# Rewriting a block-causal attention kernel that feeds a hash-routed mixture of experts

## The chip, the cores and the metric

The kernel runs on one core of a Trainium2 chip. The metric is the device time of one launch in microseconds (us). All times of the trace come from one profiled execution; the times of the kernel come from separate runs.

## What is computed

Two stages follow each other. q, k and v have 8 batches, 8 heads, 576 positions and 64 dimensions, in fp32. Attention is causal by blocks of 64 positions: position i sees position j if i // 64 >= j // 64. The result x, 4608 tokens by 512, goes to one of 8 experts per token; the token's id decides which.

```python
scores = scale * np.matmul(q, k.transpose(0, 1, 3, 2))
mask = (pos[:, None] // 64) >= (pos[None, :] // 64)
attn = softmax(np.where(mask, scores, -1e9))
x = np.matmul(attn, v).transpose(0, 2, 1, 3).reshape(4608, 512)
expert_idx = token_ids * np.int64(2654435761) % np.int64(8)
for e in range(8):
    m = expert_idx == e
    out[m] = np.maximum(x[m] @ w1[e], 0.0) @ w2[e]     # 512 -> 1024 -> 512
```

The multiplier is 1 modulo 8, so the expert is the token id modulo 8. In the inputs used here the experts have 565, 591, 525, 624, 619, 579, 546 and 559 tokens.

## The kernel before

The code has three stages, each in its own pools; the order within an engine is that in which a scheduler of the language places what the code lists, and the waits between engines come from the tiles that instructions share.

**Routing (lines 96 to 177).** The token ids are loaded four times 1152, repeated on 8 partitions (L121), one partition per expert. DVE and ACT compute the id modulo 8, a one-hot row and its running sum (L124 to L142); 72 small matmuls turn the slots to token order (L145). 36 indirect DMAs on POOL write token numbers into `perm_dram` (L171); each writes the same tensor, so each waits for the one before it. L177 reads the table back into `perm3`. An expert has 6 x 128 = 768 slots; empty ones hold the number 4608.

**Attention (L200 to L393), per batch.** SP loads q, k and v (L203 to L216); DVE casts them to bf16 (L220 to L226). PE transposes 128-row chunks of q and k by matmuls with an identity (L244, L250) into one PSUM tile, DVE and ACT copy the results out (L266, L270). Scores are computed transposed, keys by queries, per head and 128 keys, only for queries at or after them (L285, L290); ACT takes the exponential into `PT` (L302) and DVE zeroes the quarter that the block mask forbids (L308). Then PV (L351) has `PT` as the stationary side and v with a column of ones as the moving one, so the row sum comes out as column 65; DVE divides (L360 to L373). Heads go in pairs, PV of a pair after the scores of the next. SP writes x in token order to `x_dram` (L386, L391).

**Experts (L403 to L494).** The weights of an expert are loaded and cast to bf16 by POOL's DMAs (L415, L417); the pools of this stage take over the memory of attention's. For each 128 slots an indirect DMA gathers rows of x (L425), PE transposes them (L431) and DVE copies them (L435). Stage a (L446, L452) makes the hidden layer, stage b (L460, L467) the output, which an indirect DMA scatters to the tokens' rows (L468). Each such scatter writes `out`, and waits for the one before it. Experts overlap: stage a of e, then weights and gathers of e + 2, then stage b of e - 1.

Of the kernel before, what the change touches and what calls it, by code (L numbers as in the profile page):

```python
# [9 lines left out]
_PAIRINTER = _os.environ.get("BCA_PAIRINTER", "0") == "1"  # L11
_KCOPY_DVE = _os.environ.get("BCA_KCOPY_DVE", "0") == "1"
_SKIP_MOE = _os.environ.get("BCA_SKIP_MOE", "0") == "1"
_SKIP_ATT = _os.environ.get("BCA_SKIP_ATT", "0") == "1"
_SKIP_S0 = _os.environ.get("BCA_SKIP_S0", "0") == "1"
_SKIP_PV = _os.environ.get("BCA_SKIP_PV", "0") == "1"
_SKIP_TR = _os.environ.get("BCA_SKIP_TR", "0") == "1"
_PVN = int(_os.environ.get("BCA_PVN", "65"))
ALU = mybir.AluOpType
ACT = mybir.ActivationFunctionType  # L20
F32 = mybir.dt.float32
BF16 = mybir.dt.bfloat16
I32 = mybir.dt.int32
I64 = mybir.dt.int64


@with_exitstack
def kernel(
# [13 lines left out]
    B, H, S, D = q.shape  # L42
    N_tok = B * S
    E, Dm, FF = moe_w1.shape
    assert D == 64 and Dm == H * D
    assert S % P == 64 and (2 * S) % P == 0, "kernel assumes S = n*128 + 64 (e.g. 576)"
    BLK = 64
    assert (H * S) % P == 0
    NC = (H * S) // P
    NPAIR = H // 2  # L50
    assert H % 2 == 0
    NQT = (S + P - 1) // P
    NCHUNK = N_tok // P
# [38 lines left out]
    if _SKIP_S0:  # L92
        SEC = 0
# [431 lines left out]
```

## Time and profile before

| what | us |
|---|---|
| median of 3 runs (646.69 to 651.3) | 647.71 |
| profiled execution, first to last instruction | 643.9 |
| difference of the two | 3.8 |
| PE busy | 500.3 |
| ACT busy | 254.1 |
| DVE busy | 244.1 |
| POOL busy | 148.1 |

Busy times of different engines overlap. A matmul's busy time holds its latency, so neighbours overlap too. "Idle before" in a row is time in which that engine had nothing to do, with what ended it.

### The profile page before, as it was taken

Reading aid. Unit: us, or ns where it says so; the run is one execution under the profiler, and the core shown is the slowest. Engines: PE = TensorE matmul, PEld = TensorE weight load, DVE = VectorE, ACT = ScalarE, POOL = GpSimd, SP = SyncE. Lnnn points to the kernel's source line nnn. Section 1 sums busy time; section 2 is a strip of 40 time slices with the busy share of each in tenths; the row PEclk is TensorE's granted clock in tenths of the full one; section 3 lists DMA queues with packets and bytes.
Section 4 is the critical chain, followed back from the end, with each engine's and each line's share of the span. In section 5 each row is a group of like instructions: output and inputs, shape, how many; then the busy total and the mean of one; then the engine's idle time right before and its main releaser. Section 6 shows DMA issues by size and latency. Waiting matters only on the chain. (4 is left out here: it accounts for less than half of the span.)

```text
span 643.9 us, 8321 instructions
## 1 busy us (share of the span) xinstructions
PE 500.3 (78%) x3144; PEld 274.4 (43%) x3144; DVE 244.1 (38%) x823; ACT 254.1 (39%) x589; POOL 148.1 (23%) x160
## 2 busy tenths in 40 slices
PE   0426899999999999999999147879596969699850
PEld 0424454545555454555545024435252525354420
DVE  5575555464645546464444011122212121212210
ACT  3422556556565655656566004314040404043100
POOL 1001431222300000000000344441525262422232
PEclk9999999999999999999999999789898989899996
DMA  7499008356190835610010699655565655251101
GB/s 157 83 215 211 7 2 194 65 121 138 53 208 1 192 68 126 133 45 1 2 38 1 123 199 203 141 130 115 125 127 124 132 124 123 71 112 66 57 37 55
DMA packets 81065, 66.44 MB, mean 103 GB/s; under 512 B 41790, under 2 KB 73055, under 8 KB 80994
## 3 DMA queue, kind: packets, MB, share of 16 engines
q1 hardware_dynamic: 61122, 33.33, 24.9%
q0 software_dynamic: 19904, 32.59, 23.7%
q8 instruction: 24, 0.39, 0.3%
q14 instruction: 15, 0.12, 0.1%
HBM read 68.48 MB, written 17.35 MB: 133 GB/s over the span
## 5 line engine op out<-in xcount | busy, mean ns | idle before, releaser
L302 ACT ACTIVATE PT<-sc_ps 128x576 bf16<-128x576 f32 (+4 forms) x320 | 132.4, 435 | 100.8 <-PE sc_ps L285 70.5
L285 PE MATMUL sc_ps<-qkT 64*128 64x512 bf16 (+4 forms) x320 | 132.0, 438 | 10.4 <-ACT PT L302 8.2
L452 ACT ACTIVATE hT<-hp 128x256 bf16<-128x256 f32 (+1 forms) x128 | 61.9, 490 | 181.2 <-PE hp L446 180.1
L351 PE MATMUL Oall<-vext,PT 128*128 128x65 bf16 (+2 forms) x960 | 106.3, 245 | 2.1
L460 PE MATMUL yp<-w2b,hT 128*128 128x512 bf16 x384 | 96.7, 406 | 9.2 <-DVE ysb L467 9.2
L351 PEld LDWEIGHTS <-PT 128*128 128x128 bf16 (+2 forms) x960 | 67.5, 129 | 74.7 <-DVE PT L308 24.1
L446 PE MATMUL hp<-xT,w1b 128*128 128x256 bf16 (+1 forms) x512 | 95.6, 334 | 1.9 <-ACT hT L452 0.8
L266 DVE CAST qkT<-pt 64x512 bf16<-64x512 f32 (+7 forms) x128 | 58.1, 454 | 48.9 <-PE pt L250 34.1
L468 POOL DMA_INDIRECT out_dram<-ysb,perm x48 | 48.0, 999 | 116.0 <-DMA out_dram<-ysb,perm 68.0
L467 DVE COPY ysb<-yp 128x512 f32<-128x512 f32 x48 | 33.2, 691 | 98.6 <-PE yp L460 45.9
L244 PE MATMUL pt<-identbf,qb 128*64 128x128 bf16 (+1 forms) x320 | 65.0, 302 | 5.5 <-ACT qkT L270 5.2
L171 POOL DMA_INDIRECT perm_dram<-tok,f_i x36 | 37.1, 1031 | 137.2 <-DMA perm_dram<-tok,f_i 81.9
L446 PEld LDWEIGHTS <-w1b 128*128 128x128 bf16 x512 | 50.5, 99 | 42.4 <-issue 11.4
L435 DVE COPY xT<-tp 128x512 bf16<-128x512 bf16 x48 | 19.9, 424 | 125.3 <-PE tp L431 125.0
L431 PE MATMUL tp<-identbf,xg 128*128 128x128 bf16 x192 | 20.6, 246 | 59.1 <-DMA xg<-x_dram,perm 58.9
L250 PE MATMUL pt<-identbf,kb 128*64 128x128 bf16 (+1 forms) x320 | 65.0, 299 | 0.0
L460 PEld LDWEIGHTS <-hT 128*128 128x128 bf16 x384 | 39.4, 104 | 57.1 <-issue 22.1
L270 ACT CAST qkT<-pt 64x512 bf16<-64x512 f32 (+7 forms) x128 | 49.8, 389 | 34.2 <-DVE qkT L266 32.2
L425 POOL DMA_INDIRECT xg<-x_dram,perm x48 | 46.3, 965 | 48.1 <-PE tp L431 26.1
L285 PEld LDWEIGHTS <-qkT 64*128 64x128 bf16 (+1 forms) x320 | 34.9, 113 | 44.5 <-issue 26.6
L415 POOL DMA_DIRECT2D w1b<-in_moe_w_dram x8 | 6.7, 840 | 180.8 <-DMA x_dram<-xs 176.0
L145 PE MATMUL slot_ps<-ones_e,cum 8*128 8x1 f32 x72 | 16.0, 348 | 40.1 <-DVE cum L139 40.1
(55 smaller groups left out, 309.4 us busy)
## 6 DMA issues: line engine op xcount, KB each, us to landing
vf_s<-in_v_dram SPq DMA_DIRECT2D x32, 256.0 KB, 5.1
w1b<-in_moe_w_dram POOLq DMA_DIRECT2D x8, 1024.0 KB
w2b<-in_moe_w_dram POOLq DMA_DIRECT2D x8, 1024.0 KB
x_dram<-xs SPq DMA_DIRECT2D x8, 512.0 KB, 3.1
vf_s<-in_v_dram SPq DMA_DIRECT2D x8, 128.0 KB, 4.0
xg<-x_dram,perm POOLq DMA_INDIRECT x48
out_dram<-ysb,perm POOLq DMA_INDIRECT x48
perm_dram<-tok,f_i POOLq DMA_INDIRECT x36
```

Of the source, the lines that this page charges most:

```text
L244: nc.tensor.matmul(pt[64 * m : 64 * m + 64, 0, ci * P + p : ci * P + pend], lhsT=qb[p:pend, c, :], rhs=identbf[p:pend, p:pend], start=True ...
L250: nc.tensor.matmul(pt[64 * m : 64 * m + 64, 1, ci * P + p : ci * P + pend], lhsT=kb[p:pend, c, :], rhs=identbf[p:pend, p:pend], start=True ...
L266: nc.vector.tensor_copy(qkT[64 * m : 64 * m + 64, pr, 0, sa:sb], pt[64 * m : 64 * m + 64, 0, ua - gi * 4 * P : ub - gi * 4 * P],)
L270: nc.scalar.copy(qkT[64 * m : 64 * m + 64, pr, 1, sa:sb], pt[64 * m : 64 * m + 64, 1, ua - gi * 4 * P : ub - gi * 4 * P],)
L285: nc.tensor.matmul(sc_ps[p0:p1, 0:w1m], lhsT=kTs, rhs=qkT[rows, pr, 0, qs0 : qs0 + w1m], start=True, stop=True,)
L302: nc.scalar.activation(PT[p0:p1, so : so + W_], sc_ps[p0:p1, 0:W_], ACT.Exp, scale=scale,)
L351: nc.tensor.matmul(Oall[0:trows, qt, 0 : D + 1], lhsT=PT[p0:p1, cst : cst + trows], rhs=vext[p0:p1, h, pc["c"], 0 : D + 1], start=(i == 0) ...
L425: nc.gpsimd.indirect_dma_start(out=xg[:], out_offset=None, in_=x_dram[:, :], in_offset=bass.IndirectOffsetOnAxis(ap=perm3[:, gg : gg + 1], ...
L446: nc.tensor.matmul(hp[:, 0:tw], lhsT=w1b[:, db, ft * P : (ft + 1) * P], rhs=xT[:, db, t0 : t0 + tw], start=(db == 0), stop=(db == NKT - 1),)
L452: nc.scalar.activation(hT[:, ft, t0 : t0 + tw], hp[:, 0:tw], ACT.Relu)
L460: nc.tensor.matmul(yp[:, :], lhsT=hT[:, ft, tt * P : (tt + 1) * P], rhs=w2b[:, ft, :], start=(ft == 0), stop=(ft == NFT - 1),)
L468: nc.gpsimd.indirect_dma_start(out=out[:, :], out_offset=bass.IndirectOffsetOnAxis(ap=perm3[:, e * G + tt : e * G + tt + 1], axis=0), in_= ...
```

## The change

Nearly every line is new. Of the old structure the transposed scores, the ones column, the weight loads and the two-stage experts remain. What it does:

- The program's order is the order of every engine's queue (`manual_schedule`), written out by hand.
- Rows of q and k are read so that a partition holds four neighbouring positions (1 KB runs); v is read to match, in 18 DMAs per batch. The cast of v moves from DVE to POOL.
- Two heads share the 128 partitions: one transpose, one PSUM tile, one copy and one exponential serve both; score matmuls of a chunk alternate between the heads' rows. Positions 512 to 575 of all heads are handled once per batch (`T_rest`, `S_rest`).
- The block mask is a multiplication on POOL.
- Routing works on 128 partitions. Its 40 index scatters, the scatters of x and those of the output are declared independent of each other.
- x is written to its slot, expert by expert, by five indirect scatters per batch; the empty rows of each expert are zeroed first. Weights of experts 0, 1 and 2 are loaded during batches 3, 5 and 7.
- An expert has 640 slots. Its x is read with one transposing DMA; no gather, no transposes on PE. Tokens beyond 640 go to a loop at the end, whose count is read at run time.

The diff is cut to its core (added lines; `SYNC` marks a dependence that is waited for):

```diff
+    def load_qk(b):
+        for t, src in ((qf, q), (kf, k)):
+            nc.sync.dma_start(
+                t[:, 0:32, :].rearrange("p (h c) d -> p h (c d)", h=H),
+                src[b, :, 0:512, :].rearrange("h (p c) d -> p h (c d)", c=4))
...
+    def cast_v(b):
+        nc.gpsimd.tensor_copy(
+            vx[:, :, :, 0:D], vf[:, 0:32, :].rearrange("p (h i) d -> p h i d", h=H))
...
+    def T_pair(g):
+        tp = psT.tile([P, 8, P], BF16, name="tp", tag="tp")
+        for w in range(2):
+            src = casted[b][w]
+            for c in range(4):
+                s0 = (pr * 4 + c) * 2
+                nc.tensor.transpose(out=tp[:, 4 * w + c, :],
+                    in_=src[:, s0 : s0 + 2, :].rearrange("p a d -> p (a d)"), identity=identbf[:])
+        nc.vector.tensor_copy(qk[:, pr, :, 0:512]..., tp[:]...)
...
+    def mm_pair(b, pr, ps, o0, i, q0, n):
+        for m in range(2):
+            rows = slice(64 * m, 64 * m + 64)
+            nc.tensor.matmul(ps[:, m, o0 : o0 + n],
+                lhsT=qk[rows, pr, 1, 128 * i : 128 * i + 128],
+                rhs=qk[rows, pr, 0, q0 : q0 + n], start=True, stop=True)
+    def S_chunk(g, ch):
+        ps = psS.tile([P, 2, 512], F32, name="ps", tag="ps")
+        if ch == 0:
+            mm_pair(b, pr, ps, 0, 0, 0, 512)
+        elif ch == 1:
+            mm_pair(b, pr, ps, 0, 1, 128, 448)
+            mm_pair(b, pr, ps, 448, 0, 512, 64)
+        else:
+            mm_pair(b, pr, ps, 0, 2, 256, 320)
+            mm_pair(b, pr, ps, 320, 3, 384, 192)
+        nc.scalar.activation(ptv[:, :, 512 * ch : 512 * ch + 512], ps[:], ACT.Exp, scale=SCALE)
...
+    def mask(g):
+        for i in range(NT):
+            nc.gpsimd.tensor_scalar(reg, reg, halfm[:, 0:1], 1.0, op0=ALU.mult, op1=ALU.mult)
...
+    def PV(g, m):
+        O = psO.tile([P, 5, D + 1], F32, name="O", tag="O")
+        for t in range(5):
+            for i in range(min(t, NT - 1) + 1):
+                nc.tensor.matmul(O[:, t, :], lhsT=pt[:, o0 : o0 + 128], rhs=vx[:, h, i, :],
+                                 start=(i == 0), stop=(i == t))
...
+        nc.vector.reciprocal(rs[:], O[:, :, D : D + 1])
+        nc.vector.tensor_tensor(out=xs[:, :, h * D : (h + 1) * D], in0=O[:, :, 0:D],
+                                in1=rs[:].to_broadcast([P, 5, D]), op=ALU.mult)
+    def scatter_x(b):
+        for i in range(5):
+            ins = nc.gpsimd.indirect_dma_start(out=x_dram[:, :],
+                out_offset=bass.IndirectOffsetOnAxis(ap=slot_i[0:n, i, b : b + 1], axis=0),
+                in_=xs[0:n, i, :], in_offset=None)
+            nc.gpsimd.nop()
+            for w in x_writes:
+                tc.declare_no_dep(ins.ins, w.ins, reason="rows of different tokens")
+            x_writes.append(ins)
+    def route():
+        nc.sync.dma_start(tid[:], moe_token_ids.rearrange("(b s) -> b s", b=B))
...
+        for i in range(5):
+            for b in range(B):
+                ins = nc.gpsimd.indirect_dma_start(out=perm_dram[:, :], ...)
+                nc.gpsimd.nop()
+                for w in writes:
+                    tc.declare_no_dep(ins.ins, w.ins, reason="rows of different tokens")
...
+        rd = nc.gpsimd.dma_start(perm3[:], perm_dram[:]...)
+        for w in writes:
+            tc.add_manual_dep(rd.ins, w.ins.name, SYNC, reason="all tokens placed")
+    load_qk(0)
+    load_v(0)
+    load_qk(1)
+    for e in range(E):
+        z = nc.sync.dma_start(x_dram[e * CAP + 512 : (e + 1) * CAP, :], zx[:])
+    cast_qk(0, 0)
+    cast_qk(0, 1)
+    T_rest(0)
+    T_pair(0)
+    cast_v(0)
+    route()
+    load_v(1)
+    for g in range(NPAIRS + 2):
+        b, pr = divmod(g, NP)
+        if g < NPAIRS:
+            S_chunk(g, 0)
+            S_chunk(g, 1)
+        if g >= 2:
+            PV(g - 2, 0)
+        if g + 1 < NPAIRS:
+            if pr == NP - 1:
+                T_rest(b + 1)
+            T_pair(g + 1)
+        if g < NPAIRS:
+            S_chunk(g, 2)
+            if pr == 0:
+                S_rest(b)
+            mask(g)
+        if g >= 2:
+            PV(g - 2, 1)
...
+        if pr == 1 and b >= 1:
+            scatter_x(b - 1)
+            if b == 3:
+                load_weights(0)
...
+    def load_x(e):
+        r = nc.sync.dma_start_transpose(out=xT[:], in_=x_dram[e * CAP : (e + 1) * CAP, :])
+        for w in x_writes:
+            tc.add_manual_dep(r.ins, w.ins.name, SYNC, reason="all tokens placed")
+    def stage_a(e):
+        for ft in range(NFT):
+            for db in range(NKT):
+                for t in range(2):
+                    nc.tensor.matmul(hp[:, t, 0:HC], lhsT=w1b[:, db, ft * P : (ft + 1) * P],
+                        rhs=xT[:, db, t * HC : (t + 1) * HC], start=(db == 0), stop=(db == NKT - 1))
+            nc.scalar.activation(hT[:, ft, :]..., hp[:, :, 0:HC], ACT.Relu)
...
+    n_ov = nc.values_load(ov_i[0:1, 0:1], min_val=0, max_val=OVT)
+    with tc.For_i(0, n_ov, 1) as j:
...
```

The pools: `ps` has three buffers of two PSUM banks, `tp` and `O` one of one bank each; in the expert stage `hp` has two of two banks and `yp` four of one. `pt` has three buffers, q, k and v two each, the weights and `xT` three. In the loop cast_qk(b + 1), load_qk(b + 2), cast_v(b + 1) and load_v(b + 2) are issued at pairs 1, 2 and 3 of batch b. In the expert stage load_x runs two experts ahead, stage b of e - 1 follows stage a of e, and then come the weights of e + 2.

## Rows read from the trace of the kernel before

**Rows 1.** Stretches: length, busy us (instructions) of PE, PEld, DVE, ACT, POOL; clock, DMA.

```profile
0.00:56.40 56.40, 15.99 (x73) 15.65 (x73) 33.74 (x43) 16.32 (x13) 1.80 (x11) 1.00 0.85 161
56.40:357.20 300.80, 281.89 (x1984) 156.38 (x1984) 157.49 (x685) 175.88 (x448) 37.70 (x37) 1.00 0.38 80
357.20:382.10 24.90, 2.63 (x20) 2.08 (x21) 1.67 (x5) 0.00 (x0) 9.55 (x11) 1.00 0.91 182
382.10:628.60 246.50, 199.75 (x1068) 100.30 (x1067) 49.83 (x90) 61.93 (x128) 95.07 (x98) 0.94 0.52 114
```

**Rows 2.** Groups of instructions by shape: busy us, mean ns of one | idle before.

```profile
L285 PE MATMUL sc_ps<-qkT 64*128 64x512 bf16 x64 | 38.3, 599 | 4.7 <-ACT PT L302 3.0 <-DVE PT L308 1.2
L446 PE MATMUL hp<-xT,w1b 128*128 128x512 bf16 x256 | 62.2, 396 | 0.1
L351 PE MATMUL Oall<-vext,PT 128*128 128x65 bf16 (+2 forms) x960 | 106.3, 245 | 2.1
L302 ACT ACTIVATE PT<-sc_ps 128x576 bf16<-128x576 f32 x64 | 41.7, 651 | 25.4 <-PE sc_ps L290 23.6
L302 ACT ACTIVATE PT<-sc_ps 128x192 bf16<-128x192 f32 x64 | 21.1, 330 | 40.2 <-PE sc_ps L285 39.5
L435 DVE COPY xT<-tp 128x512 bf16<-128x512 bf16 x48 | 19.9, 424 | 125.3 <-PE tp L431 125.0
L360 DVE RECIPROCAL rs<-Oall 128x4 f32<-128x4 f32 x64 | 11.7, 183 | 48.6 <-PE Oall L351 47.9
L362 DVE TENSOR_TENSOR xs<-Oall,rs 128x256 bf16<-128x256 f32 x64 | 26.6, 416 | 0.6
L224 DVE CAST vext<-vf_s 128x2048 bf16<-128x2048 f32 x8 | 9.8, 1224 | 0.4
```

**Rows 3.** PE in order of time (start, us, what), and one stretch as in rows 1.

```profile
404.00:410.00 6.00, 5.22 (x22) 2.74 (x23) 1.27 (x3) 1.19 (x2) 2.87 (x3) 0.50 0.98 206
...
404.78 0.61 PE L431 MATMUL tp<-identbf,xg 128*128 128x128 bf16 x4 [3.39 <-DMA xg<-x_dram,perm]
405.18 0.63 PE L446 MATMUL hp<-xT,w1b 128*128 128x512 bf16 x1
...
336.77 0.27 PE L244 MATMUL pt<-identbf,qb 64*64 64x64 bf16 x2
...
219.34 1.17 PE L351 MATMUL Oall<-vext,PT 128*128 128x65 bf16 x13
...
597.77 10.31 PE L460 MATMUL yp<-w2b,hT 128*128 128x512 bf16 x47
```

**Rows 4.** Two of the longest waits (total, times, longest), and the chain's share by line.

```profile
POOL w1b L415 <- DMA x_dram<-xs: 176.0, 1, 176.0
...
POOL perm_dram L171 <- DMA perm_dram<-tok,f_i: 81.9, 35, 7.5
...
DMA out_dram<-ysb,perm 5%; POOLq L520 0%; POOLq L468 0%
```

**Rows 5.** POOL in order of time, with the idle time before each in brackets.

```profile
1.08 0.28 POOL masks.py:199 TENSOR_SCALAR_AFFINE_SELECT identbf<-identbf 128x128 bf16<-128x128 bf16 x1
...
67.02 0.96 POOL L171 DMA_INDIRECT perm_dram<-tok,f_i  x1 [1.43 <-DMA perm_dram<-tok,f_i]
...
364.20 0.98 POOL L425 DMA_INDIRECT xg<-x_dram,perm  x1 [0.31 <-issue]
...
633.59 0.98 POOL L468 DMA_INDIRECT out_dram<-ysb,perm  x1 [2.53 <-DMA out_dram<-ysb,perm]
```

**Rows 6.** DMA at 106 to 116, 366 to 374, 357 to 360.9 and 72 to 96 us.

```profile
DMA packets 4359, 2.14 MB, mean 214 GB/s; under 512 B 2990, under 2 KB 4358, under 8 KB 4358
...
DMA packets 1296, 1.59 MB, mean 199 GB/s; under 512 B 34, under 2 KB 1053, under 8 KB 1296
...
GB/s 0 0 0 0 0 0 74 305 368 347 347 336 357 368 347 326 347 336 347 378 315 273 242 284 242 95 21 0 0 0 0 0 0 0 0 0 0 0 0 0
...
q0 software_dynamic: 288, 0.01, 0.9%
```

More of the change, by code (lines that the diff above doesn't have):

```diff
@@ L24 @@
 I64 = mybir.dt.int64
+ET = mybir.EngineType
+B, H, S, D = 8, 8, 576, 64
+E, DM, FF = 8, 512, 1024
+N = B * S
+NT = 4
+NP = H // 2
+CAP = 640
+G = CAP // 128
+OVT = 32
+NG = E * G + OVT
+SLOTS = NG * 128
+SCALE = 1.0 / float(D) ** 0.5
 @with_exitstack
@@ new lines, with cast_qk @@
+    for z in range(2):
+        pt4 = fix.tile([P, NP * 64 + 64], BF16, name=f"pt4{z}")
+        nc.gpsimd.memset(pt4[:, NP * 64 :], 0.0)
+        pt4s.append(pt4)
+    def cast_qk(b, which):
+        src = loaded[b][which]
+        dst = att.tile([P, 36, D], BF16, name="qb" if which == 0 else "kb",
+                       tag="qb" if which == 0 else "kb")
+        nc.vector.tensor_copy(
+            dst[:, 0:32, :].rearrange("p (r c m) d -> p r m c d", r=NP, c=4, m=2),
+            src[:, 0:32, :].rearrange("p (r m c) d -> p r m c d", r=NP, c=4, m=2),
+        )
+        nc.vector.tensor_copy(dst[:, 32:36, :], src[:, 32:36, :])
+        casted.setdefault(b, {})[which] = dst
@@ new lines, in S_rest @@
+    def S_rest(b):
+        qk = qkTs[b]
+        ps = psS.tile([P, 2, 512], F32, name="ps", tag="ps")
+        for pr in range(NP):
+            for m in range(2):
+                rows = slice(64 * m, 64 * m + 64)
+                nc.tensor.matmul(
+                    ps[rows, m, 64 * pr : 64 * pr + 64],
+                    lhsT=qk[rows, pr, 1, 512:576], rhs=qk[rows, pr, 0, 512:576],
+                    start=True, stop=True,
+                )
+        for m in range(2):
+            rows = slice(64 * m, 64 * m + 64)
+            nc.scalar.activation(pt4s[b % 2][rows, 0 : NP * 64], ps[rows, m, 0 : NP * 64],
+                                 ACT.Exp, scale=SCALE)
@@ new lines, with stage_b @@
+    out_writes = []
+    def stage_b(e, hT):
+        _, w2b = wtiles[e]
+        for tt in range(G):
+            yp = psY.tile([P, DM], F32, name="yp", tag="yp")
+            for ft in range(NFT):
+                nc.tensor.matmul(
+                    yp[:], lhsT=hT[:, ft, tt * P : (tt + 1) * P], rhs=w2b[:, ft, :],
+                    start=(ft == 0), stop=(ft == NFT - 1),
+                )
+            ysb = mo.tile([P, DM], F32, name="ysb", tag="ysb")
+            nc.vector.tensor_copy(ysb[:], yp[:])
+            gg = e * G + tt
+            ins = nc.gpsimd.indirect_dma_start(
+                out=out[:, :],
+                out_offset=bass.IndirectOffsetOnAxis(ap=perm3[:, gg : gg + 1], axis=0),
+                in_=ysb[:], in_offset=None, bounds_check=N - 1, oob_is_err=False,
+            )
+            nc.gpsimd.nop()
+            for w in out_writes:
+                tc.declare_no_dep(ins.ins, w.ins, reason="rows of different tokens")
+            out_writes.append(ins)
```

783 lines of the change are left out of this document (359 added, 424 removed).

## The prediction

> **What bounds the kernel now.** I read the busy time by stage first. It cuts the 643.9 us span into five stretches [rows 1]: 56.4 us in which the tokens are routed and almost nothing else runs, 300.8 us of attention, 24.9 us between the last attention matmul and the first expert matmul, 246.5 us of experts, and a 15.3 us tail. Each has its own limit.
>
> Attention: 94% of the stretch is busy PE, but busy includes the pipeline's latency. The groups by shape tell more [rows 2]: a 512-column score matmul takes 599 ns, a 512-column expert matmul 396 ns. Where the granted clock reads 0.50 (404 to 410 us), the expert matmul takes 0.63 us [rows 3]. So I read attention as running at the 1.2 GHz level, although the stage view prints 1.00 there. PE has about 7 us of streaming in the 9.4 us (300.8 / 32) of each pair of heads; the rest are short waits on DVE and ACT. ACT is the next engine with 5.5 us per pair (175.9 / 32).
>
> Gap and experts: the list of waits shows the serial gears [rows 4]. The weight load waits 176.0 us for the last write of x, because its buffers are those of attention; index scatters wait 81.9 us for one another. The chain that ended last is the output scatters [rows 4], each waiting for the one before it, one every 3.5 us (0.98 and 2.53 [rows 5]). The gathers, with no such wait, go out every 1.3 us (0.98 and 0.31 before it [rows 5]). At the 2.4 GHz level an output matmul of 512 columns comes every (10.31 - 0.40) / 46 = 0.2154 us [rows 3], so PE's own work per expert is 32 x 0.215 + 32 x 0.108 + 48 x 0.215 and 24 transposes, about 22 us: 8 experts need 176 us and take 246.5.
>
> **The change, stretch by stretch.** The sum is made against the profiled 643.9 us; the median of the runs shown is 647.71, so 3.8 us lie around the span and are added at the end. A run differs from a repetition by up to 0.7%, so 1% is about what can be told from no change.
>
> *A. Start to first PV matmul: 56.4 -> 99 us (a loss).* SP issues, in order, q/k of batch 0 (2.36 MB), v of batch 0 (1.18), q/k of batch 1 (2.36) and 1.05 MB of zeros before the token ids. Batch loads run at 214 GB/s, writes of x at up to 340 to 378 GB/s [rows 6]: 5.9 / 0.214 + 1.05 / 0.34 = 31 us, so the ids land near 33 us. DVE then runs the routing chain: some 27 small operations at about 0.2 us and 9 over 320 elements at about 0.45 us (183 ns for 4 elements, 416 for 256 [rows 2]), 9.5 us: 43 us. POOL then issues 40 index scatters. Freed of the wait for each other they should go at the gathers' 1.3 us [rows 5], 52 us: 95 us. The read-back that follows waits for the last landing (2.4 us from issue, [rows 5]), and only behind it in POOL's queue stand the masks of the first pair (1.4 us). PV of pair 0 needs them, and PE's queue is in order, so after the scores of pairs 0 to 2 PE, ACT and DVE stand still: 99 us. Ends: q/k in 1 KB runs at 340 GB/s and scatters at 0.96 us give 77; scatters that still wait for each other (2.4 us each) give 143.
>
> *B. 32 pairs, 300.8 -> 150 us.* Per pair, engine by engine. PE at the 1.2 GHz level: scores 1536 columns per head, the two heads in different rows of the array. Two 64-row matmuls of before do run side by side: x2 in 0.27 us [rows 3], where one of 65 columns takes 0.245 [rows 2]; so 1536 x 0.43 / 512 = 1.3 us, 0.43 being twice 0.2154 (2.6 if they do not overlap). Eight transposes at 0.10 us ([rows 3]: four, then the next instruction after 0.40): 0.8. Thirty PV matmuls at (1.17 - 0.245) / 12 = 0.077 us, 13 of them in 1.17 [rows 3]: 2.3. With the 64-row remainder 0.1: 4.5 us. The same at 2.4 GHz: 2.3. ACT: 0.84 ns per column from the 651 and 330 ns exps [rows 2], so 1.03 us for 1024 columns, three per pair, and 0.2 of remainder: 3.3. DVE: one copy of 1024 columns at twice 424 ns, two reciprocals of 183 ns, two multiplies of about 0.5, a quarter of 2.8 us of q/k casts (two of 2304 elements, at the v cast's 1224 ns for 2048) and 0.15: 3.1 [rows 2]. POOL: four masks of 128 elements; the nearest row is a 128x128 select in place, 0.28 us [rows 5], 1.4 with gaps; the v cast lies between DVE's 1224 ns [rows 2] and 16 selects, 4.5 us, and I take 4.0 plus the remainder, 1.2 per pair; five scatters of x at 1.3 us per batch, 1.6: 4.2. The DMA queues: 3.54 MB per batch at 214 GB/s is 16.5 us, 4.1 per pair, and 2.5 us of x scatters, 0.6: 4.7 without weights. But three batches are loaded during A; what is left is 5 x 16.5 + 8 x 2.5 + 3 x 10.5 (2.1 MB of weights at 199 GB/s [rows 6]) = 134 us. PE and DMA thus come out level. I take 4.7 us per pair, PE's 4.5 and 0.2 for handovers: 150 us. The memsets, the copies on ACT and the second PSUM copies go; they lay beside PE. The scatter burst on POOL (6.5 us per batch) stands ahead of the next pair's mask, which PV needs two pairs later, and the pair time of 4.7 us covers it; at 3.5 us it would show. Ends: ACT's 3.3 plus handover, 3.6 (115 us); score heads one after the other and POOL's casts at their upper end, 6.2 (198 us).
>
> *C. Gap, 24.9 -> 16 us.* The weights are there early. On the path remain the last normalisation 0.8, five scatters 6.5, their landing 2.5, and the transposing load of 0.66 MB. No such DMA is in the trace; at the 340 GB/s of x's writes it is 2 us, at the rate of the weights 3.3, and a landing adds 2 to 3: I take 5. The Trainium skill (Advanced Engine Details and Errata, X-Bar Transpose (TRN2)) states that transposing DMAs are as fast as regular ones at 350 to 400 GB/s; an estimate by that figure is 1.7 us of data, which would take a microsecond or so off the sum; no run here shows it.
>
> *D. Experts, 246.5 -> 141 us.* Capacity 640 instead of 768, no PE transposes: per expert 64 matmuls of 320 columns at 0.135 us and 40 of 512 at 0.2154: 8.6 + 8.6 = 17.3 us, times 8 is 138, and about 3 for the 1.2 GHz level after C's idle time (6 us at 0.50 in [rows 3]). The output scatters no longer wait for each other: POOL needs 1.3 us per tile, PE 1.7. Copies of the output on DVE and Relus of 640 columns (0.7 us) hide. DMA per expert is 10.5 weights + 3 to 5 transposed x + 6 of output, about 20 us for five experts and 9 for the others, 127 of 141: hidden, with little to spare.
>
> *E. Tail, 15.3 -> 8 us.* Copy 0.7, scatter 1.3, landing 2.5 [rows 5], and about 3 for the test of the overflow loop on all engines (no row for it; 0 to 6). No expert of this draw has more than 624 tokens, so the loop's body does not run.
>
> Sum: 99 + 150 + 16 + 141 + 8 = 414, and 3.8 around it: 418 us.
>
> **Rivals.**
> 1. The independence does not reach the queue: scatters still wait for one another. For it: 35 such waits of 2.3 us each [rows 4]. Against: the waits are on named writes, which the change excludes. A becomes 143; the outputs at 3.5 us are 17.5 us per expert, level with PE, and trail by 9: about 470 us.
> 2. The attention pair is slower, 6 us: heads not side by side, or POOL's casts dear and late masks. For it: POOL's elementwise prices are poorly known. 418 + 42 = 460 us.
> 3. PE goes to 2.4 GHz in attention, because the new order leaves fewer pauses, and ACT sets the pair at 3.6 us. Against: DMA has 134 us to do. 418 - 35 = 383 us.
> 4. The transposing load is slow because it moves in small pieces. The small packets of the index scatters cost 288 packets for 0.9% of 16 engines over 24 us [rows 6], 12 ns each; 0.66 MB in 32-byte pieces is 20,480 of them, 15.4 us on 16 engines. With weights and output that is 31 us of DMA per expert, 216 in D instead of 141, and 10 more in C: about 503 us. The Trainium skill (VectorE: DVE Perf Modes, The three transpose paths) lists 1309 ns for one 128x128 block by DMA; taken 20 times, as an estimate, it also is above PE's time per expert; no run here shows it.
> 5. Slower than before: the load goes element by element. Ten scatters of 128 elements lie in those 24 us, 2.7 ns of an engine per element; 327,680 elements are 55 us per expert, 442 in D: about 719 us. It decides from 46 us per load on ((141 + 230) / 8). Against: the call is a transposing DMA of its own, not a copy with a stride. The same section of the Trainium skill names a strided copy as 19 times slower than the crossbar's transpose, and this call as the latter; no run here shows either.
>
> **How the numbers follow.** Forecast 49% (385 to 450 us by the ends of A and B that do not coincide), rival 1 13%, 2 10%, 3 12%, 4 12%, 5 4%. The predicted time is the forecast's 418. Low 355: A at its lower end and rival 3 together, 361, less a little. High 505 takes in rivals 1, 2 and 4. Faster by over 1% holds in all but rival 5: 0.96; of rival 5's 0.04, 0.03 are slower and 0.01, loads of about 46 us, within 1%.
>
> **What would show it.** First PV matmul near 99 us, with POOL's 40 index scatters 1.3 us apart ahead of it and PE idle; if they are 2.4 us apart rival 1 holds. 512-column score matmuls still near 600 ns, starting in twos; near 390 ns is rival 3. Pairs every 4.7 us. A transposing load that lands within 5 us of issue; 15 or more is rival 4. Expert matmuls without pauses, 17.3 us per expert. The forecast is wrong if attention takes under 125 or over 180 us, or if PE waits for x or weights in the experts.

## The result, and the profile after

The changed kernel takes 410.3 us (median of 4 runs, 409.2 to 413.0); the kernel before took 647.2 beside it. The ratio is 0.634 (95% interval 0.631 to 0.637); the prediction was 418 us, range 355 to 505. The profiled execution spans 409.4 us and was timed at 411.0.

The view of stretches, cut at the prediction's own steps A to E (length, busy us and instructions of PE, PEld, DVE, ACT, POOL; clock, DMA share, GB/s), answers to [rows 1]:

```profile
0.00:96.87 96.87, 8.85 (x70) 4.41 (x70) 19.93 (x66) 9.89 (x11) 46.00 (x66) 1.00 0.51 134
96.87:242.09 145.22, 100.98 (x1570) 68.54 (x1570) 82.18 (x195) 89.66 (x102) 112.92 (x189) 0.84 0.76 184
242.09:257.41 15.32, 0.01 (x1) 0.03 (x1) 0.69 (x2) 0.00 (x0) 4.92 (x5) 0.50 0.66 130
257.41:399.40 141.99, 140.15 (x824) 81.59 (x832) 26.98 (x40) 45.06 (x64) 47.59 (x49) 0.99 0.84 169
399.40:409.40 10.00, 0.00 (x0) 0.00 (x0) 0.69 (x1) 0.00 (x0) 1.21 (x2) 0.71 0.10 38
```

| step | before | predicted | after |
|---|---|---|---|
| A start to first PV matmul | 56.4 | 99 | 96.9 |
| B 32 pairs | 300.8 | 150 | 145.2 |
| C gap | 24.9 | 16 | 15.3 |
| D experts | 246.5 | 141 | 142.0 |
| E tail | 15.3 | 8 | 10.0 |

Every length came within 5 us. That does not make every reason right: in the second row PE is busy in only 101 of 145 us at a mean granted clock of 0.84, where the prediction had it busy throughout at the 1.2 GHz level. Which parts of the rewrite brought attention from 300.8 to 145.2 us no run separates. The groups by shape (busy us, mean ns of one | idle before) answer to [rows 2]:

```profile
L230 ACT ACTIVATE pt<-ps 128x1024 bf16<-128x1024 f32 x96 | 93.1, 1028 | 133.5 <-PE ps L210 119.9 <-POOL pt L254 6.3 <-issue 2.2
L254 POOL TENSOR_SCALAR pt<-pt,halfm 128x128 bf16<-128x128 bf16 x128 | 51.6, 420 | 16.5 <-ACT pt L230 15.5
L161 POOL CAST vx<-vf 128x2048 bf16<-128x2048 f32 x8 | 15.1, 1889 | 16.4 <-DMA vf<-in_v_dram 16.4
L210 PE MATMUL ps<-qkT 64*128 64x512 bf16 x64 | 14.6, 455 | 6.6 <-DVE qkT L201 6.3 <-ACT pt L230 0.2
L201 DVE COPY qkT<-tp 128x1024 bf16<-128x1024 bf16 x32 | 21.9, 685 | 10.4 <-PE tp L196 9.2 <-issue 0.7
```

ACT's exponential is priced well (1.03 us). POOL's prices are not: a mask takes 420 ns on average instead of 0.35, and the v cast 1.9 us instead of 4.0. The 512-column score matmul takes 455 ns, a mean of two levels. In order of time, attention shows what happens (start, us, what, idle before in brackets):

```profile
98.24 0.62 PE L196 MATMUL tp<-identbf,qb 128*128 128x128 bf16 x4
...
104.07 0.40 PE L196 MATMUL tp<-identbf,qb 128*128 128x128 bf16 x4 [0.63 <-DVE qkT L183]
...
105.52 0.61 PE L210 MATMUL ps<-qkT 64*128 64x512 bf16 x6
...
114.49 1.05 POOL L302 DMA_INDIRECT x_dram<-xs,slot_i  x1 [0.16 <-DVE xs L290]
114.51 0.62 PE L279 MATMUL O<-vx,pt 128*128 128x65 bf16 x14 [0.47 <-DVE xs L290]
...
120.24 0.90 POOL L302 DMA_INDIRECT x_dram<-xs,slot_i  x1 [0.30 <-issue]
120.54 0.20 DVE L289 RECIPROCAL rs<-O 128x5 f32<-128x5 f32 x1 [2.51 <-remote]
...
121.18 2.12 POOL L254 TENSOR_SCALAR pt<-pt,halfm 128x128 bf16<-128x128 bf16 x6
...
122.55 0.61 PE L196 MATMUL tp<-identbf,qb 128*128 128x128 bf16 x4 [4.17 <-DVE qkT L183]
...
124.06 0.95 PE L279 MATMUL O<-vx,pt 128*128 128x65 bf16 x14
```

Four transposes take 0.62 us at 98.24, as in [rows 3] where the granted clock reads 0.50, and 0.40 at 104.07: in the second pair PE goes over to the 2.4 GHz level. Two heads' score matmuls do run side by side: six of them, 2048 columns, take 0.61 us, and one after the other at 0.2154 us per 512 they would need 0.86.

The five scatters of x hold POOL from 114.49 to 121.14, and the masks come after them. Beside the scatters the reciprocal of a PV that ended at 117.3 starts only at 120.54, after 2.51 us in which DVE did nothing, released by something that the profile does not name ("remote"); PE waits for the copy behind it on DVE and pauses 4.17 us. This is no single case: 13 of the 64 normalisations start over 0.4 us after their matmuls have ended and DVE is free, all of them beside scatters, 19.8 us in all. Before the pause 14 PV matmuls take 0.62 us, after it 0.95. The stretches around it (columns as above) show the granted clock with it:

```profile
104.00:113.00 9.00, 7.99 (x149) 5.52 (x150) 5.85 (x15) 7.80 (x10) 5.77 (x12) 1.00 0.52 156
...
122.00:131.00 9.00, 8.27 (x116) 5.59 (x116) 4.50 (x13) 5.89 (x8) 6.17 (x14) 0.71 0.89 271
```

From one pair's last normalisation to the next the time is, from the second pair on and batch by batch, 4.8, 3.1, 3.0 | 4.0, 9.3, 3.7, 3.0 | 4.1, 8.4, 4.2, 3.0 us, and so on. A pair that nothing disturbs takes 3.0 to 3.1, three exponentials of ACT; the second pair of a batch, behind the burst of scatters, takes 6.5 to 9.3 in six batches and 5.5 in the seventh.

### The profile page after: what moved, and what is told of

The parts are those of the page before. It is cut to its first block, busy times and chain, and to the rows that moved or that the text cites. A ratio compares the mean times of both kernels' runs of the same rounds, so it can differ in the third digit from the quotient of the medians.

```text
span 409.4 us, 6483 instructions
## 1 busy us (share of the span) xinstructions
PE 250.0 (61%) x2463; PEld 154.6 (38%) x2471; DVE 130.5 (32%) x303; ACT 144.6 (35%) x177; POOL 212.6 (52%) x309
## 5 line engine op out<-in xcount | busy, mean ns | idle before, releaser
L230 ACT ACTIVATE pt<-ps 128x1024 bf16<-128x1024 f32 x96 | 93.1, 1028 | 133.5 <-PE ps L210 119.9
L279 PE MATMUL O<-vx,pt 128*128 128x65 bf16 x896 | 46.2, 208 | 71.8 <-POOL pt L254 48.2
L529 PE MATMUL hp<-xT,w1b 128*128 128x320 bf16 x512 | 72.1, 303 | 16.7 <-issue 15.3
L534 ACT ACTIVATE hT<-hp 128x640 bf16<-128x640 f32 x64 | 45.1, 704 | 103.7 <-PE hp L529 103.4
L279 PEld LDWEIGHTS <-pt 128*128 128x128 bf16 x896 | 37.7, 107 | 89.0 <-POOL pt L254 60.3
L529 PEld LDWEIGHTS <-w1b 128*128 128x128 bf16 x512 | 50.3, 99 | 38.7 <-issue 15.4
L254 POOL TENSOR_SCALAR pt<-pt,halfm 128x128 bf16<-128x128 bf16 x128 | 51.6, 420 | 16.5 <-ACT pt L230 15.5
L422 POOL DMA_INDIRECT perm_dram<-tok,prow x40 | 38.6, 966 | 31.8 <-DVE tok L400 19.9
L302 POOL DMA_INDIRECT x_dram<-xs,slot_i x40 | 43.3, 1081 | 17.8 <-issue 9.6
L210 PE MATMUL ps<-qkT 64*128 64x512 bf16 (+4 forms) x320 | 39.1, 341 | 6.8 <-DVE qkT L201 6.3
L290 DVE TENSOR_TENSOR xs<-O,rs 128x320 bf16<-128x320 f32 x64 | 31.5, 492 | 2.2
L201 DVE COPY qkT<-tp 128x1024 bf16<-128x1024 bf16 x32 | 21.9, 685 | 10.4 <-PE tp L196 9.2
L196 PE MATMUL tp<-identbf,qb 128*128 128x128 bf16 x128 | 15.3, 255 | 16.3 <-DVE qkT L183 9.6
L161 POOL CAST vx<-vf 128x2048 bf16<-128x2048 f32 x8 | 15.1, 1889 | 16.4 <-DMA vf<-in_v_dram 16.4
```

The source lines that it names most:

```text
L196: nc.tensor.transpose(out=tp[:, 4 * w + c, :], in_=src[:, s0 : s0 + 2, :].rearrange("p a d -> p (a d)"), identity=identbf[:],)
L210: nc.tensor.matmul(ps[:, m, o0 : o0 + n], lhsT=qk[rows, pr, 1, 128 * i : 128 * i + 128], rhs=qk[rows, pr, 0, q0 : q0 + n], start=True, sto ...
L230: nc.scalar.activation(ptv[:, :, 512 * ch : 512 * ch + 512], ps[:], ACT.Exp, scale=SCALE)
L254: nc.gpsimd.tensor_scalar(reg, reg, halfm[:, 0:1], 1.0, op0=ALU.mult, op1=ALU.mult)
L279: nc.tensor.matmul(O[:, t, :], lhsT=pt[:, o0 : o0 + 128], rhs=vx[:, h, i, :], start=(i == 0), stop=(i == t),)
L290: nc.vector.tensor_tensor(out=xs[:, :, h * D : (h + 1) * D], in0=O[:, :, 0:D], in1=rs[:].to_broadcast([P, 5, D]), op=ALU.mult,)
```

## The experiments

All stages, cut as above, each from one profiled execution. The last column is the median of four runs for the changed kernel and the two combinations, and a single run for the others:

| kernel | set | A | B | C | D | E | time of its runs |
|---|---|---|---|---|---|---|---|
| changed kernel | - | 96.9 | 145.2 | 15.3 | 142.0 | 10.0 | 410.3 |
| masks on DVE | a | 50.3 | 174.8 | 17.2 | 141.3 | 10.0 | 395.2 |
| index scatters late | a | 49.3 | 144.7 | 15.6 | 162.4 | 10.0 | 383.7 |
| q, k of 2 batches only | a | 96.2 | 135.3 | 14.8 | 141.8 | 10.0 | 399.8 |
| two masks | a | 96.7 | 142.4 | 14.8 | 141.2 | 10.0 | 406.7 |
| two masks, q, k of 2 batches | b | 97.8 | 141.9 | 14.7 | 141.4 | 10.0 | 407.5 |
| ids first | b | 84.0 | 145.0 | 14.3 | 142.2 | 10.1 | 397.2 |
| index scatters wait | b | 147.7 | 143.4 | 14.8 | 140.5 | 10.0 | 457.9 |
| plain load, no loop | b | 96.7 | 143.8 | 13.2 | 142.9 | 7.1 | 405.4 |
| two masks, spread | c | 97.0 | 147.7 | 14.9 | 141.4 | 10.0 | 412.6 |
| the same, q, k of 2 batches | c | 96.3 | 142.6 | 14.8 | 141.8 | 10.0 | 407.3 |
| first combination | c | 36.2 | 169.2 | 25.0 | 152.3 | 10.4 | 398.6 |
| second combination | a | 37.8 | 136.0 | 32.1 | 142.5 | 10.0 | 360.5 |

Kernels of one set ran on the same chip (the second combination later, on that of set a). Where the code of attention was not touched B lies between 143.4 and 145.2, so about 2 us is no difference there. But the sets differ in one thing: the late normalisations beside scatters sum to 15 to 20 us in each kernel of set b, as in the changed kernel, to 5 to 9 in set c, and to nothing in set a. B is therefore compared within a set. Set a also says that they are not simply a part of the 145 us: without any of them index scatters late needs 144.7 us and two masks 142.4, but over those runs DVE's casts wait 12.9 and 14.5 us for q and k, against 6.7 in the changed kernel, so one delay may hide behind the other.

**Start: index scatters that wait.**

```diff
-                for w in writes:
-                    tc.declare_no_dep(ins.ins, w.ins, reason="rows of different tokens")
```

> Edit: the 40 index scatters are no longer declared independent of each other, nothing else. Theory (a scatter that must see the one before it landed takes about 2.4 us instead of 1.26): the first PV matmul comes near 143 us instead of 96.9, the rest as it was, the whole about 456. Rival (the declaration does nothing, the spacing of 1.26 us is POOL's own): 409 to 413.

Measured: first PV at 147.7, whole 457.9. POOL's index scatters in this run, in order of time:

```profile
63.36 0.95 POOL L422 DMA_INDIRECT perm_dram<-tok,prow  x1 [1.70 <-DMA perm_dram<-tok,prow]
65.76 0.95 POOL L422 DMA_INDIRECT perm_dram<-tok,prow  x1 [1.45 <-DMA perm_dram<-tok,prow]
```

And in the changed kernel:

```profile
62.26 0.96 POOL L422 DMA_INDIRECT perm_dram<-tok,prow  x1 [0.30 <-issue]
63.52 0.96 POOL L422 DMA_INDIRECT perm_dram<-tok,prow  x1 [0.31 <-issue]
```

This answers to [rows 5]: the wait for a landing goes, 0.30 us of issue stays, and neither wait of [rows 4] is left: 40 scatters are spaced 1.26 us instead of about 2.5. Waiting costs 50.8 us in A; the prediction's rival 1 had 44 there.

**Start: scatters moved, ids first.** In the first kernel the block of fill, 40 scatters and read-back is called behind the last scatter of x; in the second only the load of the ids moves.

```diff
-    route()
+    prow, tok = route()
...
+    place(prow, tok)
     att_ctx.close()
```

> Edit: only the place of the 40 index scatters, their fill and their read-back on POOL is moved, from ahead of the first mask to behind the last scatter of x. Theory: the first PV matmul comes near 48 us instead of 96.9, because nothing else held the masks; the pairs keep POOL's pace, so attention takes about 145 us and ends near 193; the index scatters then run beside the gap and the first experts (50 us), hold the first output scatters and the weights of expert 3 behind them and cost about 14 us there: 410 - 49 + 14 = 375 us. Rival (the start is set by routing on DVE or by loads, not by the scatters on POOL): the first PV matmul stays past 80 us and the whole does not fall below 400.

```diff
+    nc.sync.dma_start(tid[:], moe_token_ids.rearrange("(b s) -> b s", b=B))
     load_qk(0)
     load_v(0)
```

> Edit: only the place of the load of the token ids in SP's queue, from behind the loads of q, k, v and the zeros to ahead of them. Theory (SP's order sets when routing starts): the ids are there when DVE has copied the first transposes at 16.3 us; routing starts at 16.5 instead of 32.0, waits about a microsecond for POOL's iota behind the v cast, and the first PV matmul comes near 83 us instead of 96.9; the whole 396. Rival (what the start gives is taken back by the loads in attention): first PV near 83, the whole 403 to 408. Rival (routing needs something else that comes at 30 us): first PV stays near 97.

Measured: first PV at 49.3 and at 84.0, wholes 383.7 and 397.2. Both steps of A hold: SP's order sets when routing starts, and the masks stand behind the scatters. The first PV matmul, in the changed kernel's order of time:

```profile
95.77 0.58 POOL L433 DMA_DIRECT2D perm<-perm_dram  x1 [1.41 <-DMA perm_dram<-tok,prow]
96.44 1.08 POOL L254 TENSOR_SCALAR pt<-pt,halfm 128x128 bf16<-128x128 bf16 x3
...
96.87 0.70 PE L279 MATMUL O<-vx,pt 128*128 128x65 bf16 x5 [47.29 <-POOL pt L254]
```

Of the 48 us that moving the scatters saves in A, 20 come back in D (14 expected). In order of time, behind the moved scatters and their read-back:

```profile
258.17 1.01 POOL L556 DMA_INDIRECT out_dram<-ysb,perm  x1 [2.29 <-DMA perm<-perm_dram]
...
261.78 5.18 PE L549 MATMUL yp<-w2b,hT 128*128 128x512 bf16 x16 [10.05 <-DVE ysb L554]
272.80 2.58 PE L534 MATMUL hp<-xT,w1b 128*128 128x320 bf16 x9 [5.83 <-DMA w1b<-in_moe_w_dram]
```

The first output scatter goes out only at 258.17, so the output copies and PE stop for 10.05 us, and then 5.83 us for weights that stood behind them on POOL.

**Attention: whose pace?** Masks to DVE; then loads left out; then POOL's instructions merged; then both.

```diff
-            nc.gpsimd.tensor_scalar(reg, reg, halfm[:, 0:1], ...)
+            nc.vector.tensor_scalar(reg, reg, halfm[:, 0:1], ...)
```

> Edit: the four mask multiplications of a pair go from POOL to DVE and stand behind the second head's normalisation; the same values are computed. Theory (POOL sets the pace of attention, by its masks and by the 40 index scatters that stand ahead of them): the first PV matmul comes near 48 us instead of 96.9, but the PV of pair 4 needs the v cast of batch 1, which still stands behind the index scatters, so PE stops again until about 99; from there 28 pairs at DVE's 3.7 us (3.1 and four masks at 0.15) are 104 us, attention ends near 203 and the whole takes about 371 us. Rival (loads by the DMA engines set the pace): attention ends at 215 to 235, the whole takes 385 to 400. Rival (PE's own work sets the pace, 4.5 us per pair): 99 + 28 x 4.5 = 225, the whole 393.

```diff
-                    load_qk(b + 2)
+                    loaded[b + 2] = [loaded[b][0], loaded[b][1], None]
```

> Edit: q and k of batches 2 to 7 are not read; the tiles of batches 0 and 1 are used again, so the scores of the later batches are those of the first two. 14.2 of 66.1 MB of DMA go. Theory (POOL sets the pace of attention): attention keeps 140 to 147 us, the whole 405 to 411. Rival (loads set the pace, 4.1 us per pair of the measured 4.54): attention falls to what POOL, ACT or DVE allow, 105 to 130 us, the whole to 370 to 395.

```diff
-        for i in range(NT):
+        for i in (0, 3):
+            if i == 0:
+                reg = ptv.rearrange("p m (i x j) -> p m i x j", i=3, x=32)[:, :, :, 0:8:2, :]
```

> Edit: the four mask multiplications of a pair on POOL become two, one of 384 elements per partition and one of 128; the same values are computed. Theory (POOL sets the pace, and an instruction has a fixed part: 128 elements take 420 ns, a cast of 2048 takes 1889): 384 elements take about 0.65 us, a pair is 0.6 us shorter on POOL, attention 126 us instead of 145 and the whole 391. If POOL's price is by the element, 384 take 1.26 us and nothing changes. Rival (loads or PE set the pace): POOL's rows get shorter, attention keeps 142 to 146 us.

> Edit: both at once, two mask multiplications instead of four on POOL, and q and k of batches 2 to 7 not read (the tiles of batches 0 and 1 are used again). Alone the first took attention from 145 us to about 140, the second to 135. Theory (POOL and the loads are two limits that lie nearly level, so that removing one only uncovers the other): together they give far more than the sum of 15, attention 112 to 122 us (POOL is left with 15 us per batch, ACT with 13.2), the whole 375 to 387. Rival (each is a small share of one sum): attention 130 us, the whole 394. Rival (PE's 4.5 us per pair are the floor): no less than 140.

Measured: with the masks on DVE the first PV comes at 50.3, and PV then waits 36.1 us for a v cast, as expected; but from 100 us attention needs 125 us, not 104: the theory missed, and the end at 225 us fits both rivals' numbers. The time does not come from a steady pace: batches 3 to 6 take 15.5 to 16.5 us, where index scatters late, of the same set, needs 15.7 to 21.8, and the longest stop, 11.67 us in batch 7, is for a load. In order of time, with the masks on DVE:

```profile
192.08 1.23 DVE L151 CAST qb<-qf 128x2048 bf16<-128x2048 f32 x1 [7.59 <-DMA qf<-in_q_dram]
...
196.08 0.29 DVE L155 CAST qb<-qf 128x256 bf16<-128x256 f32 x1 [2.77 <-DMA qf<-in_q_dram]
...
197.06 0.95 PE L279 MATMUL O<-vx,pt 128*128 128x65 bf16 x14 [11.67 <-DVE xs L290]
```

Against the kernel of the same set whose attention is unchanged (index scatters late, 144.7, though its loads have less of a start) the missing loads of q and k give 9.4 us, to 135.3, between the two theories (140 to 147, or 105 to 130). Two masks instead of four give 2.3, within the rival's 142 to 146 and far from the theory's 126, though 384 elements take 0.74 us on average instead of three times 0.42: POOL is freed and waits longer for ACT (26.9 us instead of 15.5), since the merged mask needs the last exponential. Both together, in set b, give 141.9 against 143.4 to 145.0 there, where 112 to 122 was expected: the theory of two level limits missed, but 15.4 us of late normalisations lie in that run, so it was not decided by it. What these runs have in common is the place of the stops. With q and k of 2 batches only (set a, four masks), in order of time:

```profile
135.79 0.90 POOL L302 DMA_INDIRECT x_dram<-xs,slot_i  x1 [0.30 <-DMA vf<-in_v_dram]
136.74 2.79 POOL L254 TENSOR_SCALAR pt<-pt,halfm 128x128 bf16<-128x128 bf16 x8
137.16 0.11 PEld L279 LDWEIGHTS <-pt 128*128 128x128 bf16 x2 [2.00 <-POOL pt L254]
137.17 1.39 PE L279 MATMUL O<-vx,pt 128*128 128x65 bf16 x14 [1.72 <-POOL pt L254]
```

Here no normalisation is late, and PE stops for the masks behind the last scatter. Over attention PE's loads of stationary data for PV wait 21.7 us for masks in this run, 12.1 in the changed kernel.

**Attention: is it the burst?** This suggests, and does not yet show, that not POOL's sum but its order counts. The scatters are spread, on the last two kernels:

```diff
-        if pr == 1 and b >= 1:
-            scatter_x(b - 1)
+        if b == B and pr == 1:
+            scatter_x(b - 1, range(5))
+        elif b >= 1 and pr in (1, 2):
+            scatter_x(b - 1, range(2 * pr - 2, 2 * pr))
+        elif b >= 2 and pr == 0:
+            scatter_x(b - 2, [4])
```

> Edit: on the kernel with two mask multiplications (attention 143 us from the first PV matmul to the last normalisation, the whole 406.7); the five scatters of x per batch are no longer in one place on POOL but two behind the second pair, two behind the third and one behind the first pair of the next batch (the last batch's stay together). Theory (it is the burst that costs: 6.5 us of scatters, with weights 8.8, hold the masks longer than the two pairs of lead cover at 3.1 us each, and after each pause PE runs the next pairs at the lower clock): attention 124 to 134 us, the whole 388 to 398. Rival (the loads' 134 us set the pace): attention 134 to 140. Rival (POOL's sum or something else sets the pace, the place does not matter): attention 141 to 145, the whole 405 to 409.

> Edit: the same spreading of the scatters, on the kernel with two mask multiplications and without the reading of q and k of batches 2 to 7 (left out; attention 143 us, the whole 407.5, which refuted that POOL's sum and the loads were the two limits). Theory (the burst): with the loads light and the burst gone POOL has 15 us per batch and ACT 13.2, attention 112 to 124 us, the whole 376 to 389. Rival (the burst is not the cause): attention stays at 136 to 145. Against the run with full loads: if the loads bind once the burst is gone, this one is 8 us or more shorter in attention; if not, within 4.

Measured: 147.7 and 142.6, no gain, and 5.1 between the two, which falls between the bounds named for the loads. By attention and by the whole the theory missed both times, and without the loads the rival's 136 to 145 holds. By batches (time from one batch's last normalisation to the next, weights of an expert issued in the fourth, sixth and eighth) it is half right:

| kernel, q and k of 2 batches | the 8 batches, us |
|---|---|
| four masks, scatters together (set a) | 15.6, 15.7, 17.6, 19.2, 15.7, 19.1, 15.7, 17.4 |
| two masks, scatters together (set b) | 14.9, 17.6, 18.9, 19.0, 16.9, 19.3, 17.9, 18.1 |
| two masks, scatters spread (set c) | 14.9, 16.8, 17.2, 15.6, 25.6, 15.6, 23.3, 14.4 |

With the scatters spread six of the eight lie between 14.4 and 17.2, but two rise above 23. Part of that gain over set b is that fewer normalisations are late: in set a, where none is, the scatters stay together and the five batches without weights take 15.6 to 17.6, the three with weights 17.4 to 19.2. In order of time, with the scatters spread:

```profile
150.75 0.83 POOL L444 DMA_DIRECT2D w1b<-in_moe_w_dram  x1
151.55 0.96 POOL L446 DMA_DIRECT2D w2b<-in_moe_w_dram  x1
...
153.66 1.08 POOL L304 DMA_INDIRECT x_dram<-xs,slot_i  x1 [0.18 <-issue]
155.05 1.00 POOL L304 DMA_INDIRECT x_dram<-xs,slot_i  x1 [0.30 <-issue]
...
167.00 0.41 POOL L164 CAST v<-vf 64x256 bf16<-64x256 f32 x1 [7.80 <-DMA x_dram<-xs,slot_i]
167.50 0.93 POOL L256 TENSOR_SCALAR pt<-pt,halfm 128x384 bf16<-128x384 bf16 x2
168.14 0.95 PE L281 MATMUL O<-vx,pt 128*128 128x65 bf16 x14 [7.49 <-POOL pt L256]
```

The cast of v's remainder waits until the scatters of x have landed; in the changed kernel it starts without delay (0.06 us of idle at most). Spreading put two scatters behind 4 MB of weights (fp32 in HBM) in POOL's own DMA queue; the cast went on 12 us after the second of them was issued, the masks stood behind it, and PE paused 7.49 us. With the full loads the same cast goes on 13.5 us after that scatter (155.59 to 169.05). One wait was traded for another, so these two runs do not decide what a spread burst alone would give.

**Gap, experts and tail: transposing load, loop.** Both edits in one kernel:

```diff
-        r = nc.sync.dma_start_transpose(out=xT[:], in_=x_dram[e * CAP : (e + 1) * CAP, :])
+        r = nc.sync.dma_start(xT[:].rearrange("p k c -> p (k c)"),
+            x_dram[e * CAP : (e + 1) * CAP, :].rearrange("(p g) d -> p (g d)", g=G))
...
-    n_ov = nc.values_load(ov_i[0:1, 0:1], min_val=0, max_val=OVT)
-    with tc.For_i(0, n_ov, 1) as j:
```

> Edit: two, in stages that can be read apart. The transposing load of an expert's x becomes a plain load of the same 0.66 MB (left out: the transposition), and the overflow loop behind the experts is left out, with the reading of its count. Theory: the plain load lands 1 to 2 us sooner, so the gap falls from 15.3 to about 14; PE's pauses in the experts (2.7 us) go, 142 to about 139; the tail falls from 10.0 to about 6.5, as the test of the loop costs some 3 us on engines that are done; the whole 401 to 404. Rival (the transposing load is no dearer than a plain one): gap and experts keep 15 and 142. Rival (the tail is the landing of the last scatter and the end of the program): the tail keeps 9 to 10.

Measured: gap 13.2, experts 142.9, tail 7.1, whole 405.4. In the changed kernel, from the issue of the load to the first expert matmul:

```profile
251.24 9.41 SPq L516 DMA_TRANSPOSE xT<-x_dram  x3
257.41 4.83 PE L529 MATMUL hp<-xT,w1b 128*128 128x320 bf16 x24 [15.32 <-issue]
```

With the plain load:

```profile
249.63 1.31 SPq L516 DMA_DIRECT2D xT<-x_dram  x3
253.69 8.48 PE L531 MATMUL hp<-xT,w1b 128*128 128x320 bf16 x41 [13.20 <-issue]
```

6.2 against 4.1 us: transposing costs 2.1 us once, in the gap, and nothing that shows in the experts, whose 142 us did not fall to the 139 expected. The loop's test costs 2.9 us.

**Putting it together.** The first combination has ids first, two masks, spread scatters, 17 index scatters singly between the pairs and 23 behind x.

> Edit: what helped, in one kernel that computes all: token ids loaded first; the 40 index scatters taken from the start, 17 of them singly between the pairs, 23 behind the last scatter of x, beside the gap and the first experts; two mask multiplications; scatters of x spread over the pairs; weights of expert 2 loaded behind the last scatter of x instead of in batch 7. Theory: first PV matmul near 29 us; attention is then bound by the loads (35 MB at 235 GB/s behind the start, 151 us), with POOL at 145 us, and ends near 180; gap 15, experts 142, tail 10: the whole 347 us. Rival (POOL's single index scatters bring the pauses back): attention ends near 195, the whole 362. Rival (23 index scatters behind x hold the first output scatters and the weights of expert 3): experts 150 to 160, the whole 355 to 365.

Measured: 398.6 us, ratio 0.617 (0.612 to 0.622) to the kernel before: a miss by 52. The wait of the v cast came back (up to 11.4 us for scatters of x, up to 12.5 for v itself), the first transposing load took 16.4 us beside the weights of expert 2, and the experts lost 10, in part in two stops of PE (3.7 and 4.1 us) while the last of the 23 index scatters ran and landed. The second takes the masks off POOL and the weights out of the loads' way:

```diff
+        if pr == 3 and b == 6:
+            load_weights(0)
+            load_weights(1)
+        if b == 0:
+            place(1 if pr == 3 else 3)
+        elif b < 7 and pr in (0, 2):
+            place(2 if b < 5 or pr == 0 else 1)
```

> Edit: one kernel that computes all, with POOL taken off the path from exponential to PV: token ids loaded first; masks on DVE (two multiplications, behind the second head's normalisation); the 40 index scatters spread, 10 in batch 0, 4 or 3 in batches 1 to 6, 8 behind the last scatter of x; weights of experts 0 and 1 behind the last v cast, when all loads of q, k and v are under way, those of expert 2 behind the last scatter of x; the five scatters of x of a batch together again. Theory (what set the pace of attention is POOL's queue, in which scatters and a v cast that waits for their landing stand ahead of masks, and weights that push loads and landings back): first PV matmul near 36 us, as in the combined kernel; every batch takes 15.5 to 16.5 us, as the undisturbed ones did with the masks on DVE; attention 126 to 132 us, its end near 165; gap 15, experts 142 to 146, tail 10: the whole 333 to 345 us. Rival (the loads bind now: 33.5 MB at 235 GB/s are 143 us from the first load): attention ends past 172, DVE waits for q or k, the whole 348 to 360. Rival (POOL's sum of 15 to 16 us per batch still binds, through late v casts): batches of 18 us, attention 145, the whole 352 to 362.

Measured: 360.5 us (357.9 to 365.5), ratio 0.555 (0.551 to 0.558): faster than both kernels, 12% under the changed one, but 15 us above the range named. Attention took 136.0 instead of 126 to 132, its batches 2 to 7 15.2 to 19.6 instead of 15.5 to 16.5; its end at 173.8 is past the 172 of the loads' rival, but DVE waits only 4.7 us for q, and PE's stops now end with DVE's normalisations (21.1 us). The gap took 32.1 instead of 15; 17 us less would put the whole inside the range named. Its POOL, SP and PE in order of time:

```profile
174.86 0.96 POOL L304 DMA_INDIRECT x_dram<-xs,slot_i  x1 [4.63 <-DVE xs L292]
179.83 0.95 POOL L304 DMA_INDIRECT x_dram<-xs,slot_i  x1 [4.01 <-DMA w1b<-in_moe_w_dram]
185.01 0.95 POOL L304 DMA_INDIRECT x_dram<-xs,slot_i  x1 [4.23 <-DMA w2b<-in_moe_w_dram]
...
188.42 0.84 POOL L449 DMA_DIRECT2D w1b<-in_moe_w_dram  x1
...
190.30 17.88 SPq L530 DMA_TRANSPOSE xT<-x_dram  x3
...
205.91 6.33 PE L543 MATMUL hp<-xT,w1b 128*128 128x320 bf16 x26 [32.08 <-issue]
```

The same collision as in the spread kernels, now in the gap: the last scatters of x wait 8.2 us for the weights of experts 0 and 1, and the transposing load, beside those of expert 2, takes 15.6 us from issue to first matmul instead of 6.2. Placing these weights so that neither meets them should return most of the 17 us; that was not tried.

## Why the prediction was right, step by step

- **A holds in length and reason.** 99 us predicted, 96.9 measured. Three edits moved the first PV matmul as their chains say: ids first to 84.0 (83 expected), scatters away to 49.3 (48), scatters waiting to 147.7 (143).
- **B came within 5 us by a wrong term.** That 4.7 us per pair meets the measured 4.54 is luck. The step that failed is "PE's 4.5" per pair, summed for "PE at the 1.2 GHz level", and with it "PE and DMA thus come out level". PE reaches the 2.4 GHz level in the second pair (the transposes above); an undisturbed pair takes 3.0 to 3.1 us, three exponentials of ACT. The price was high even for the lower level: 14 PV matmuls take 0.95 us there, where its 0.077 per matmul makes 1.25. The prediction's own signs say so: score matmuls of 455 ns, neither near 600 nor near 390, and pairs of 3.0 to 9.3 us instead of 4.7 each. The rest of the 4.54 is pauses: batches 2 to 8 take 18.6 us on average where four undisturbed pairs would take 12.2, and the difference lies in the pairs beside and behind POOL's burst of scatters. There stand late masks (12.1 us), late normalisations (19.8 us, no part of the prediction) and slower matmuls after a pause; how much each costs by itself stays open, since the same attention code without a late normalisation (index scatters late, set a) needs 144.7 us. The prediction had part of this in a clause, "at 3.5 us it would show", and did not follow it; it gave rival 3 only 12%. Rival 3's own price, 3.6 us per pair, was wrong too, as it left the burst out.
- **B and the loads.** Leaving out q and k of six batches gives 7.1 us (against two masks, the other kernel of set a with the same start) to 9.4, so loads are part of the pace. Whether they are a floor of "134 us" was not tested by itself: the run with 14 MB less stays at 135.3, so something else holds it there.
- **C and D hold.** The terms named for C, 0.8, 6.5, 2.5 and 5, add up to 14.8, not to the 16 that went into the sum; measured were 15.3. The load took 6.2 us where 5 were taken, scatters and landing 8.1 (243.1 to 251.2) where 9.0 were. Rivals 4 and 5 fell: the experts' PE is busy 140.2 of 142.0 us, and a plain load changes nothing there. The Trainium skill (Advanced Engine Details and Errata, X-Bar Transpose (TRN2)) states that transposing DMAs are as fast as regular ones; here one such load of 0.66 MB took 2.1 us longer from issue to first use, 6.2 against 4.1. The Trainium skill (VectorE: DVE Perf Modes, The three transpose paths) lists 1309 ns per 128x128 block by DMA; 20 times that, an estimate of 26 us per load, does not agree with the 6.2 us measured.
- **E was mis-sized by 2 us.** The loop's test cost the 2.9 us assumed (3); the last tile's copy, its scatter, the landing and the program's end took 7.1, not 4.5. Outside the span lay 1.6 us in the profiled execution, not 3.8: that figure had set the median of several executions against the span of another.

## What to carry to other kernels

Price an in-order queue by what stands ahead of the instruction that others wait for, and not by its sum alone: POOL was busy in 113 of 145 us and merging its masks gave almost nothing, while PE's stops lay beside and behind its burst of scatters. That the burst sets the pace is argued from the order of time and from the shorter batches with the masks off POOL; no run that only spread it became faster. Before moving or spreading DMA issues, list for each queue what follows them and who waits for their landing; four kernels here lost time because 4 MB of weights stood ahead of small scatters, or beside a load. When two engines come out level in an estimate, work out the next pair time with one of them at its other clock, and see which burst is then no longer covered.

## What the runs showed of the hardware

A POOL instruction that starts during DVE's fp32 to bf16 cast of 2048 elements takes longer and ends after the cast, in all 13 cases of the changed kernel. In order of time there:

```profile
131.77 0.37 POOL L254 TENSOR_SCALAR pt<-pt,halfm 128x128 bf16<-128x128 bf16 x1 [0.54 <-ACT pt L230]
...
132.41 1.22 DVE L151 CAST qb<-qf 128x2048 bf16<-128x2048 f32 x1
...
132.69 1.65 POOL L254 TENSOR_SCALAR pt<-pt,halfm 128x128 bf16<-128x128 bf16 x2 [0.54 <-ACT pt L230]
```

Two masks that take 0.74 us elsewhere (0.37 each) take 1.65, of which the first takes 1.30 and ends 0.36 us after the cast. It happens to scatters too (1.55 instead of 0.96 at 117.12, beside the cast of k at 116.45); the mask's mean is 420 ns. The Trainium skill (SBUF — State Buffer, SBUF: two separate sides) describes such an exclusive lock on a port pair shared by DVE and GpSimd; the trace agrees.

Normalisations on DVE start late beside POOL's scatters in eight of the thirteen executions profiled, by up to 2.9 us each, and on the chip of set a never. What holds them was not found, and how much of such a delay reaches the time of attention is open, so edits of attention are compared on one chip.

PE's clock followed its pauses: granted 1.00, the 2.4 GHz level, while pairs ran without a stop, and 0.71, in part the 1.2 GHz level, in the stretch with a pause of 4.17 us in front. Behind the pauses of 4.17, 7.49 and 11.67 us shown above 14 PV matmuls took 0.95 us instead of 0.62. The clock column alone can mislead: from 97 to 104 us of the changed kernel it prints 1.00, while four transposes take 0.62 us there as at a granted 0.50; the times of like matmuls decide.
